# Loading the second attention tile ahead of the weights, by halves of the heads, in a fused attention and MLP kernel

## The chip, the cores and the metric

The kernel runs on one core of a Trainium2 chip. The time is device microseconds of one execution; medians over several executions are given. In the profile PE is the engine of matrix products (PEld its weight loads), DVE, ACT and POOL are the vector, scalar and general engines, and SP issues DMAs.

## The reference

```python
scores = (q @ k.T) / sqrt(64)              # q, k, v: [4, 8, 768, 64], float32
# retrieval heads: causal mask; others: causal and (first 4 keys or last 64 keys)
a = softmax(where(mask, scores, -1e9))
x = (a @ v) as [3072, 512]                 # the heads side by side
h = x @ w_in                               # [512, 2048]
out = (h - tanh(h)) @ w_out                # [2048, 512] -> [3072, 512]
```

## The kernel before

The 3072 tokens are cut into 12 tiles of 256. A tile has four head pairs. For each pair: transposes of q and k (`tp`), copies of them (`qT`, and two `kz`), scores (`sc`), exp (`pt`), a mask multiply with `m`, the product with v (`av`), a division (`x`), a transpose back (`xp`) and a copy (`xT`). A bank in the code is one of a few output buffers of PE that the steps use in turn. Then come the tile's MLP (the two products with `w_in` and `w_out`), `ph` (with `w_in`), `th`, `gt` and `po` (with `w_out`), with the attention of later tiles in its gaps. All instructions are recorded with an estimated cost, and a planner in the kernel (`Plan`) simulates them to choose a fixed order for each engine.

```python
    def load(t, names="qkv"):                  # SP queue: q, k, v of tile t
        ...
            for i in range(NB):                # NB = 2 blocks of 128 tokens
                op("SP", 420, lambda ...: nc.sync.dma_start(
                        out=r()[:, i, :, :],
                        in_=src[b, :, s0 : s0 + 128, :].rearrange("h p d -> p h d")),
                    w=[("raw", idx, i)], dma=(1024, 21.0))
    def load_w_in(j):                          # POOL queue: fp32 to fp16 on the way
        ...
            r=[("v1", 0, 0)], w=[("win", j)], dma=(512, 80.0))
    def load_w_out(j):
        ...
            r=[("v1", 0, W_OUT_AFTER)], w=[("wout", j)], dma=(512, 80.0))
    # ... cut: constants, masks m4, casts, scores, av
    def st_X(n):
        ...
        xp, key = bank([128, NB, 128], FP16, "m", f"xp{n}")   # av uses "m" too: one bank
    # ... cut: MLP units
    cast_qk(0, (("DVE", "DVE"), ("DVE", "ACT")))
    cast_v(0)
    for j in range(4):
        load_w_in(j)
    scale_v(0)
    load(1)
    for n in range(HP):                        # the four head pairs of tile 0
        st_T(n, "ACT", ("DVE", "DVE"))
        # ... cut: scores, av and xp of the pairs before
    cast_qk(1, (("DVE", "DVE"), ("DVE", "POOL")))
    cast_v(1)
    scale_v(1)
    for j in range(4):
        load_w_out(j)
    load(2)
```

The softmax here doesn't subtract the row's maximum and nothing guards it: scores larger than these inputs give would overflow.

Of the kernel before, what the change touches and what calls it, by code (L numbers as in the profile page):

```python
# [7 lines left out]
FP32 = mybir.dt.float32  # L8
# [4 lines left out]
TT = 256  # L13
# [3 lines left out]
class Plan:  # L17
# [15 lines left out]
    def op(self, eng, ns, fn, r=(), w=(), dma=None, prio=None):  # L33
# [18 lines left out]
        self.ops.append((eng, ns, fn, deps, dma, i if prio is None else prio))  # L52
        return i

    def run(self):
# [15 lines left out]

        def enqueue(i):
            queue[self.ops[i][0]].append(i)

        def finish(i, done):
            self.done[i] = done
            e, ns, _, _, dma, _ = self.ops[i]
# [14 lines left out]
        while len(order) < n:  # L92
            t, e = min(
                [(max(free[e], min(ready[i] for i in q)), e) for e, q in queue.items() if q],
# [18 lines left out]
            elif nxt < t:  # L113
# [4 lines left out]
                (i for i in queue[e] if ready[i] <= t), key=lambda i: self.ops[i][5]  # L118
            )
            queue[e].remove(i)  # L120
            _, ns, _, _, dma, _ = self.ops[i]
            self.start[i] = t
            order.append(i)
            free[e] = t + max(ns - self.OVERLAP[e], 40)
            if dma:
                packets, each = dma
                rings["POOL" if e == "POOL" else "SP"].append(
                    [i, t + ns + 300, each, packets * each / 16]
                )
            else:  # L130
                finish(i, t + ns + self.RESULT[e])
# [6 lines left out]
def kernel(  # L138
# [86 lines left out]
    def load(t, names="qkv"):  # L225
        b, g = divmod(t, NG)
        for nm in names:
            src = {"q": q, "k": k, "v": v}[nm]
            idx = 3 * t + "qkv".index(nm)
            r = lazy(raw_pool, [128, NB, H, D], FP32, "raw", f"raw_{nm}{t}")  # L230
            for i in range(NB):
                s0 = g * TT + i * 128
                op(
                    "SP", 420,
                    lambda r=r, i=i, src=src, s0=s0: nc.sync.dma_start(
                        out=r()[:, i, :, :],
                        in_=src[b, :, s0 : s0 + 128, :].rearrange("h p d -> p h d"),
                    ),
                    w=[("raw", idx, i)], dma=(1024, 21.0),
                )  # L240
            raws[nm, t] = (r, idx)

    W_OUT_AFTER = 2
# [3 lines left out]
    def load_w_in(j):  # L247
# [7 lines left out]
            r=[("v1", 0, 0)], w=[("win", j)], dma=(512, 80.0),  # L255
# [3 lines left out]
    def load_w_out(j):  # L259
# [7 lines left out]
            r=[("v1", 0, W_OUT_AFTER)], w=[("wout", j)], dma=(512, 80.0),  # L267
# [12 lines left out]
    load(0, "qk")  # L280
    load(0, "v")
# [80 lines left out]
    for h in range(H):  # L362
# [6 lines left out]
            r=["thr", "A4", "A40", "A41", "A43"], w=[("m4", h // 2)],  # L369
# [15 lines left out]
    def cast_qk(t, engines):  # L385

        for nm, es in zip("qk", engines):
            c = lazy(t16_pool, [128, NB, H, D], FP16, f"t16{nm}", f"t16_{nm}{t}")
            r, slot = raws[nm, t]
            for i, e in enumerate(es):  # L390

                def fn(c=c, r=r, i=i, e=e):
                    if e == "ACT":
                        nc.scalar.copy(out=c()[:, i, :, :], in_=r()[:, i, :, :])
                    else:
                        engs[e].tensor_copy(out=c()[:, i, :, :], in_=r()[:, i, :, :])  # L396

                op(
                    e, {"ACT": 590, "DVE": 380, "POOL": 540}[e], fn,
                    r=[("raw", slot, i)], w=[("t16" + nm, t, i)],  # L400
                )
            t16s[nm, t] = c
# [4 lines left out]
    def cast_v(t):  # L407
        b, g = divmod(t, NG)
        if g == 0:
            v1s[b] = lazy(v_pool, [128, 2 * NG, H, D + 1], FP16, "v1", f"v1_{b}")  # L410
            vfs[b] = lazy(v_pool, [128, 4, H, D + 1], FP16, "vf", f"vf_{b}")
        v1, vf, lo = v1s[b], vfs[b], g * NB
        r, slot = raws["v", t]
        op(
            "POOL", 200,
            lambda: nc.gpsimd.memset(v1()[:, lo : lo + NB, :, D : D + 1], 1.0 / XS),
            w=[("v1", b, lo + i) for i in range(NB)],
        )
        for i in range(NB):
            op(  # L420
                "POOL", 540,
                lambda i=i: nc.gpsimd.tensor_copy(  # L422
                    out=v1()[:, lo + i, :, 0:D], in_=r()[:, i, :, :]
                ),
                r=[("raw", slot, i)], w=[("v1", b, lo + i)],
            )

    def scale_v(t):
        b, g = divmod(t, NG)
        v1, vf, lo = v1s[b], vfs[b], g * NB  # L430
        for jb in range(lo, min(lo + NB, 4)):
# [7 lines left out]
                r=[("v1", b, jb), "rflag0", "rflag"], w=[("vf", b, jb)],  # L439
# [6 lines left out]
    xTs = {}  # L446

    def st_T(n, eq="DVE", ek=("DVE", "DVE")):
# [6 lines left out]
        def mm():  # L455
# [9 lines left out]
            r=["ident"] + [("t16" + nm, t, i) for nm in "qk" for i in range(NB)], w=[key],  # L465
        )
        qT[n] = lazy(qt_pool, [128, TT], FP16, f"qT{hp}", f"qT{n}")

        def copy(e, dst, src):
            if e == "ACT":  # L470
                nc.scalar.copy(out=dst, in_=src)  # L471
            else:
                nc.vector.tensor_copy(out=dst, in_=src)  # L473
# [33 lines left out]
    def st_S(n, gi):  # L507
# [35 lines left out]
        if gi == 0:  # L543
# [15 lines left out]
            op("DVE", 560 if g == 0 else 695, mask, r=pk + [("m4", hp)], w=pk)  # L559
# [3 lines left out]
    def st_A(n, i):  # L563
# [20 lines left out]
        r += [("v1", b, jb) for jb in range(max(qb - 1, 0), qb + 1)]  # L584
# [20 lines left out]
    def st_X(n):  # L605
# [3 lines left out]
        xp, key = bank([128, NB, 128], FP16, "m", f"xp{n}")  # L609

        def mm():
            for i in range(NB):
# [6 lines left out]
            "DVE", 290,  # L619
            lambda: nc.vector.tensor_copy(  # L620
                out=xTs[t]()[:, hp, :], in_=xp()[:].rearrange("p i c -> p (i c)")
            ),
# [103 lines left out]

    cast_qk(0, (("DVE", "DVE"), ("DVE", "ACT")))
    cast_v(0)
    for j in range(4):
        load_w_in(j)  # L730
    scale_v(0)
    load(1)
# [100 lines left out]
```

## Time and profile before

| | before |
|---|---|
| median of 3 runs (range) | 276.85 us (276.75 to 277.22) |
| profiled span | 275.6 us |
| PE busy / idle | 251.2 / 24.4 us |
| PE idle from 0 to 48 us | 18.8 us |
| first w_in issued; last w_out landed | 10.44; 48.2 us |
| first `ph` | 23.94 us |
| last `xp` of tile 1 | 46.91 us |

The stage table, the timeline (start, duration, engine, line, operation, count; in brackets the idle time ahead of it and what ended it) and the queue rows are in the prediction below. These are PE rows of the timeline of the kernel before (start, duration, engine, line, operation, count; in brackets the idle time ahead of it and what ended it):

```profile
39.72 0.19 PE L578 MATMUL av<-vf,pt 128*128 128x65 f16 x1 [0.90 <-DVE xT L620]
...
46.91 0.29 PE L613 MATMUL xp<-ident,x 128*128 128x128 f16 x2 [0.73 <-DVE x L597]
```

Tile 1's attention, which waits on DVE for each pair, then has little beside it to fill PE: tile 0's `ph` is over by 36.3 us, and only `po` rows, from 40.91 on, stand between its pairs.

### The profile page before, as it was taken

To read this page: it belongs to the slowest core of one execution; us is meant where nothing else is said; L and a number is where in the kernel's file an instruction comes from. 1 tells how busy PE (TensorE), PEld (TensorE's weight loads), DVE (VectorE), ACT (ScalarE), POOL (GpSimd) and SP (SyncE) were. 2 spreads that over 40 slices of the span, in tenths; PEclk is the share of its full clock that TensorE was granted. 3 is DMA by queue.
4 is the path that set the end of the run, shared out by engine and by line. 5 is a ranking of instruction groups with operands and counts; after the bars stand their busy time and mean duration, and the time that the engine had idled before them with its cause. 6 is when DMAs were issued, how large, how long until landed. Compare 5 with 4: busy or idle time off the path is not lost.

```text
span 275.6 us, 6251 instructions
## 1 busy us (share of the span) xinstructions
PE 251.2 (91%) x2560; PEld 186.9 (68%) x2560; DVE 179.6 (65%) x452; ACT 154.2 (56%) x223; POOL 69.5 (25%) x116
## 2 busy tenths in 40 slices
PE   0457977999999999999999999999999999999984
PEld 0335764888778777777777777777777877776631
DVE  7784775776898875556987655567987655554310
ACT  2330464788357676665476776564567566644420
POOL 7530940527190730206803000300300000000000
PEclk9999999999999999999999999999999999999999
DMA  7999999999989590182860210010001001011101
GB/s 140 217 199 209 191 207 203 221 220 232 230 177 201 129 224 32 40 190 66 201 144 15 76 43 4 37 40 38 2 38 40 2 38 40 1 40 39 40 38 76
DMA packets 82733, 29.78 MB, mean 108 GB/s; under 512 B 75536, under 2 KB 79632, under 8 KB 82704
## 3 DMA queue, kind: packets, MB, share of 16 engines
q1 hardware_dynamic: 78336, 25.17, 41.7%
q0 software_dynamic: 4224, 4.19, 9.2%
q8 instruction: 20, 0.33, 0.5%
q14 instruction: 9, 0.07, 0.1%
q10 hardware_dynamic: 144, 0.01, 0.0%
HBM read 27.27 MB, written 6.29 MB: 122 GB/s over the span
## 4 chain that ended last, share of the span: by engine, by line
PE 84%; DVE 11%; ACT 2%; issue 2%
PE ph L642 29%; PE po L678 29%; PE sc L522 13%; PE av L578 8%; PE tp L458 3%; PE xp L613 2%; DVE x L597 1%; DVE kz L473 1%; DVE gt L662 1%; DVE pt L554 1%; DVE pt L549 1%; DVE kz L331 1%; DVE m L365 1%; DVE xT L620 1%; ACT th L655 1%
## 5 line engine op out<-in xcount | busy, mean ns | idle before, releaser
L642 PE MATMUL ph<-xT,win 128*128 128x256 f16 x768 | 103.3, 278 | 0.7 <-DVE gt L662 0.7
L678 PE MATMUL po<-wout,gt 128*128 128x512 f16 x384 | 100.0, 379 | 1.4 <-ACT ot L691 1.4
L537 ACT ACTIVATE pt<-sc 128x1024 f16<-128x1024 f32 (+1 forms) x96 | 85.5, 916 | 23.7 <-PE sc L522 19.4
L655 ACT ACTIVATE th<-ph 128x512 f32<-128x512 f32 x96 | 57.4, 598 | 71.4 <-PE ph L642 67.5
L662 DVE SCALAR_TENSOR_TENSOR gt<-th,ph 128x512 f16<-128x512 f32 x96 | 65.8, 686 | 38.6 <-ACT th L655 38.1
L642 PEld LDWEIGHTS <-win 128*128 128x128 f16 x768 | 73.8, 100 | 16.3 <-issue 1.1
L522 PE MATMUL sc<-qT,kz 128*128 128x128 f16 (+1 forms) x448 | 53.2, 250 | 2.5 <-DVE kz L473 2.0
L678 PEld LDWEIGHTS <-gt 128*128 128x128 f16 x384 | 34.2, 98 | 23.3 <-issue 1.9
L522 PEld LDWEIGHTS <-kz 128*128 128x128 f16 x448 | 37.0, 99 | 14.1 <-DVE kz L473 2.8
L578 PEld LDWEIGHTS <-pt 128*128 128x128 f16 x672 | 30.1, 98 | 9.6 <-issue 2.1
L396 POOL CAST t_q<-raw_q 128x512 f16<-128x512 f32 x20 | 12.4, 646 | 90.3 <-PE tp L458 47.5
L578 PE MATMUL av<-v,pt 128*128 128x65 f16 x352 | 29.3, 196 | 1.5 <-DVE xT L620 0.8
L473 DVE COPY kz<-tp 64x256 f16<-64x256 f16 x96 | 27.1, 283 | 3.4 <-ACT qT L471 1.2
L554 DVE TENSOR_TENSOR pt<-pt,m 128x1024 f16<-128x1024 f16 x32 | 23.3, 729 | 4.7 <-ACT pt L537 4.7
L578 PE MATMUL av<-vf,pt 128*128 128x65 f16 x320 | 23.5, 193 | 1.6 <-DVE xT L620 0.9
L458 PE MATMUL tp<-ident,t_q 128*128 128x128 f16 x96 | 13.8, 226 | 9.2 <-DVE t_q L396 8.8
L691 ACT ACTIVATE ot<-po 128x512 f32<-128x512 f32 x24 | 14.4, 598 | 12.9 <-PE po L678 12.7
L597 DVE TENSOR_TENSOR x<-av,rinv 128x256 f16<-128x256 f32 x48 | 20.3, 423 | 1.5
L592 DVE RECIPROCAL rinv<-av 128x4 f32<-128x4 f32 x48 | 8.7, 180 | 17.7 <-PE av L578 17.2
L422 POOL CAST v<-raw_v 128x512 f16<-128x512 f32 x24 | 15.0, 641 | 18.7 <-DMA raw_v<-in_v_dram 18.5
L435 POOL TENSOR_TENSOR vf<-v,rflag 128x520 f16<-128x520 f16 x16 | 18.2, 1146 | 0.7
L458 PEld LDWEIGHTS <-t_q 128*128 128x128 f16 x96 | 8.8, 101 | 13.4 <-DVE t_q L396 8.9
(35 smaller groups left out, 121.7 us busy)
## 6 DMA issues: line engine op xcount, KB each, us to landing
raw_q<-in_q_dram SPq DMA_DIRECT2D x24, 256.0 KB, 4.9
raw_k<-in_k_dram SPq DMA_DIRECT2D x24, 256.0 KB, 4.8
raw_v<-in_v_dram SPq DMA_DIRECT2D x24, 256.0 KB, 4.9
out_dram<-ot SPq DMA_DIRECT2D x24, 256.0 KB, 2.1
win<-in_moe_w_in_dram POOLq DMA_DIRECT2D x4, 512.0 KB, 10.4
wout<-in_moe_w_out_dram POOLq DMA_DIRECT2D x4, 512.0 KB, 10.6
retr_i<-in_is_retrieval_dram ACTq DMA_DIRECT2D x1, 8.0 KB, 3.1
```

The source lines that it names most:

```text
L435: lambda jb=jb, fl=fl: nc.gpsimd.tensor_mul(out=vf()[:, jb, :, :], in0=v1()[:, jb, :, :], in1=fl[:].unsqueeze(2).to_broadcast([128, H, D + ...
L458: nc.tensor.transpose(out=tp()[:, x, i, :], in_=c()[:, i, 2 * hp : 2 * hp + 2, :], identity=ident16[:],)
L473: nc.vector.tensor_copy(out=dst, in_=src)
L522: nc.tensor.matmul(out=sc()[:, hh, o : o + nb * 128], lhsT=kk[:, hh, jb * 128 : jb * 128 + 128], rhs=qT[n]()[:, q0 * 128 : (q0 + nb) * 128 ...
L537: lambda: nc.scalar.activation(out=pt()[:, :, 512 * gi : 512 * gi + wid], in_=sc()[:, :, 0:wid], func=AF.Exp, scale=inv_sqrt_d,),
L554: nc.vector.tensor_mul(out=pv, in0=pv, in1=m4[:, hs, 256:512].unsqueeze(2).to_broadcast([128, 2, 2, 256]),)
L578: nc.tensor.matmul(out=av()[:, i, hh, :], lhsT=pt()[:, hh, co : co + 128], rhs=vv()[:, jb, h, :], start=(jb == 0), stop=(jb == qb),)
L597: lambda: nc.vector.tensor_mul(out=x16()[:], in0=av()[:, :, :, 0:D], in1=rinv()[:].unsqueeze(3).to_broadcast([128, NB, 2, D]),),
L642: nc.tensor.matmul(out=ph()[:, j, :], lhsT=w_in_t[fb // 4]()[:, cb, f0 : f0 + 128], rhs=xTs[t]()[:, cb, :], start=(cb == 0), stop=(cb == H ...
L655: lambda: nc.scalar.activation(out=th()[:], in_=ph()[:], func=AF.Tanh, scale=1.0 / XS),
L662: lambda: nc.vector.scalar_tensor_tensor(out=gts[t]()[:, u * FU : (u + 1) * FU, :], in0=th()[:], scalar=-XS, in1=ph()[:], op0=ALU.mult, op ...
L678: nc.tensor.matmul(out=po()[:], lhsT=gts[t]()[:, f, ts * 128 : ts * 128 + 128], rhs=w_out_t[f // 4]()[:, f % 4, :], start=(f == 0), stop=( ...
```

## The change

The intent is that PE should have two tiles' attention to work on before the MLP starts. Tile 1's q, k, v are requested, moved and cast before the weights; loads and casts go by halves of the heads, so that the first pairs can start on half a tile; two copies move to ACT; `xp` of tile 0 uses the bank `o`, idle until the first `po`. The planner also learns that DVE and POOL share a port.

```diff
-    def load(t, names="qkv"):
+    def load(t, names="qkv", halves=(None,)):
     ...
-            r=[("v1", 0, 0)], w=[("win", j)], dma=(512, 80.0),
+            r=w_after, w=[("win", j)], dma=(512, 80.0),
     ...
-    load(0, "qk")
-    load(0, "v")
+    for half in range(2):
+        load(0, "qk", (half,))
+        load(0, "v", (half,))
     ...
-    cast_qk(0, (("DVE", "DVE"), ("DVE", "ACT")))
-    cast_v(0)
-    for j in range(4):
-        load_w_in(j)
-    scale_v(0)
-    load(1)
+    cast_qk(0, (("DVE", "DVE"), ("ACT", "DVE")), (0,))
+    cast_v(0, ("POOL", "POOL"), (0,))
+    cast_qk(0, (("DVE", "DVE"), ("DVE", "DVE")), (1,))
+    cast_v(0, ("POOL", "POOL"), (1,))
+    load(1, halves=range(2))
     for n in range(HP):
-        st_T(n, "ACT", ("DVE", "DVE"))
+        st_T(n, "ACT", ("DVE", "ACT"))
     ...
-            st_X(n - 3)
+            st_X(n - 3, "o")
     ...
-    cast_qk(1, (("DVE", "DVE"), ("DVE", "POOL")))
-    cast_v(1)
+    for half in range(2):
+        cast_qk(1, (("POOL", "POOL"), ("ACT", "POOL")), (half,))
+        cast_v(1, ("POOL", "POOL"), (half,))
+    for j in range(4):
+        load_w_in(j, [("t16k", 1, 1)])
+    load(2)
+    scale_v(0)
     scale_v(1)
     for j in range(4):
-        load_w_out(j)
-    load(2)
+        load_w_out(j, [("v1", 0, 1, 1)])
```

Cut: the planner's port, and the bookkeeping of halves.

More of the change, by code (lines that the diff above doesn't have):

```diff
@@ L31, in __init__, with op @@
         self.readers = {}
-    def op(self, eng, ns, fn, r=(), w=(), dma=None, prio=None):
+    def op(self, eng, ns, fn, r=(), w=(), dma=None, prio=None, port=False):
         i = len(self.ops)
@@ L51, in op @@
         deps.discard(i)
-        self.ops.append((eng, ns, fn, deps, dma, i if prio is None else prio))
+        port = port or (eng == "POOL" and not dma)
+        self.ops.append((eng, ns, fn, deps, dma, i if prio is None else prio, port))
         return i
@@ L70, in run, with at @@
         order = []
+        self.port = 0.0
+        def at(i):
+            return max(ready[i], self.port) if self.ops[i][6] else ready[i]
         def enqueue(i):
@@ L76, in finish @@
             self.done[i] = done
-            e, ns, _, _, dma, _ = self.ops[i]
+            e, ns = self.ops[i][:2]
             for u in users[i]:
@@ L93, in run @@
             t, e = min(
-                [(max(free[e], min(ready[i] for i in q)), e) for e, q in queue.items() if q],
+                [(max(free[e], min(at(i) for i in q)), e) for e, q in queue.items() if q],
                 default=(1e12, None),
@@ L117, in run @@
             i = min(
-                (i for i in queue[e] if ready[i] <= t), key=lambda i: self.ops[i][5]
+                (i for i in queue[e] if at(i) <= t), key=lambda i: self.ops[i][5]
             )
             queue[e].remove(i)
-            _, ns, _, _, dma, _ = self.ops[i]
+            _, ns, _, _, dma, _, port = self.ops[i]
             self.start[i] = t
@@ L124, in run @@
             free[e] = t + max(ns - self.OVERLAP[e], 40)
+            if port:
+                self.port = free[e]
             if dma:
@@ L223, with load_w_in @@
     raws = {}
-    def load(t, names="qkv"):
+    HH = H // 2
+    def load(t, names="qkv", halves=(None,)):
         b, g = divmod(t, NG)
-        for nm in names:
-            src = {"q": q, "k": k, "v": v}[nm]
-            idx = 3 * t + "qkv".index(nm)
-            r = lazy(raw_pool, [128, NB, H, D], FP32, "raw", f"raw_{nm}{t}")
-            for i in range(NB):
-                s0 = g * TT + i * 128
-                op(
-                    "SP", 420,
-                    lambda r=r, i=i, src=src, s0=s0: nc.sync.dma_start(
-                        out=r()[:, i, :, :],
-                        in_=src[b, :, s0 : s0 + 128, :].rearrange("h p d -> p h d"),
-                    ),
-                    w=[("raw", idx, i)], dma=(1024, 21.0),
-                )
-            raws[nm, t] = (r, idx)
-    W_OUT_AFTER = 2
+        for half in halves:
+            h0, nh = (0, H) if half is None else (half * HH, HH)
+            for nm in names:
+                src = {"q": q, "k": k, "v": v}[nm]
+                if (nm, t) not in raws:
+                    idx = rot["raw"] = rot.get("raw", -1) + 1
+                    raws[nm, t] = (
+                        lazy(raw_pool, [128, NB, H, D], FP32, "raw", f"raw_{nm}{t}"), idx
+                    )
+                r, idx = raws[nm, t]
+                for i in range(NB):
+                    s0 = g * TT + i * 128
+                    op(
+                        "SP", max(420, 128 * nh * 1.1),
+                        lambda r=r, i=i, src=src, s0=s0, h0=h0, nh=nh: nc.sync.dma_start(
+                            out=r()[:, i, h0 : h0 + nh, :],
+                            in_=src[b, h0 : h0 + nh, s0 : s0 + 128, :].rearrange("h p d -> p h d"),
+                        ),
+                        w=[("raw", idx, i, x) for x in (range(2) if half is None else (half,))],
+                        dma=(128 * nh, 21.0),
+                    )
     w_in_t = []
     w_out_t = []
-    def load_w_in(j):
+    def load_w_in(j, w_after):
         w = lazy(w_pool, [128, HP, 512], FP16, f"win{j}", f"win{j}")
@@ L254, in load_w_in, with load_w_out @@
             ),
-            r=[("v1", 0, 0)], w=[("win", j)], dma=(512, 80.0),
+            r=w_after, w=[("win", j)], dma=(512, 80.0),
         )
         w_in_t.append(w)
-    def load_w_out(j):
+    def load_w_out(j, w_after):
         w = lazy(w_pool, [128, 4, DM], FP16, f"wout{j}", f"wout{j}")
@@ L266, in load_w_out @@
             ),
-            r=[("v1", 0, W_OUT_AFTER)], w=[("wout", j)], dma=(512, 80.0),
+            r=w_after, w=[("wout", j)], dma=(512, 80.0),
         )
@@ L368 @@
             ),
-            r=["thr", "A4", "A40", "A41", "A43"], w=[("m4", h // 2)],
+            r=["thr", "A4", "A40", "A41", "A43"], w=[("m4", h // 2)], port=True,
         )
@@ L383, with cast_op @@
     t16s = {}
-    def cast_qk(t, engines):
-        for nm, es in zip("qk", engines):
-            c = lazy(t16_pool, [128, NB, H, D], FP16, f"t16{nm}", f"t16_{nm}{t}")
-            r, slot = raws[nm, t]
-            for i, e in enumerate(es):
-                def fn(c=c, r=r, i=i, e=e):
-                    if e == "ACT":
-                        nc.scalar.copy(out=c()[:, i, :, :], in_=r()[:, i, :, :])
-                    else:
-                        engs[e].tensor_copy(out=c()[:, i, :, :], in_=r()[:, i, :, :])
-                op(
-                    e, {"ACT": 590, "DVE": 380, "POOL": 540}[e], fn,
-                    r=[("raw", slot, i)], w=[("t16" + nm, t, i)],
+    def cast_op(e, ns, dst, src, r, w):
+        cost = {"ACT": 163 + 0.85 * ns, "DVE": 85 + 0.65 * ns, "POOL": 90 + 0.96 * ns}[e]
+        if e == "ACT":
+            op(e, cost, lambda: nc.scalar.copy(out=dst(), in_=src()), r=r, w=w)
+        else:
+            op(e, cost, lambda: engs[e].tensor_copy(out=dst(), in_=src()), r=r, w=w, port=True)
@@ new lines, in cast_qk @@
+    def cast_qk(t, engines, halves=range(2)):
+        for half in halves:
+            for nm, es in zip("qk", engines):
+                if (nm, t) not in t16s:
+                    t16s[nm, t] = lazy(
+                        t16_pool, [128, NB, H, D], FP16, f"t16{nm}", f"t16_{nm}{t}"
+                    )
+                c = t16s[nm, t]
+                r, slot = raws[nm, t]
+                hs = slice(half * HH, half * HH + HH)
+                cast_op(
+                    es[half], NB * HH * D, lambda c=c, hs=hs: c()[:, :, hs, :],
+                    lambda r=r, hs=hs: r()[:, :, hs, :],
+                    r=[("raw", slot, i, half) for i in range(NB)], w=[("t16" + nm, t, half)],
@@ L401, in cast_qk, with cast_v @@
                 )
-            t16s[nm, t] = c
     v1s = {}
     vfs = {}
-    def cast_v(t):
+    def cast_v(t, engines=("POOL", "POOL"), halves=range(2)):
         b, g = divmod(t, NG)
-        if g == 0:
+        lo = g * NB
+        if b not in v1s:
             v1s[b] = lazy(v_pool, [128, 2 * NG, H, D + 1], FP16, "v1", f"v1_{b}")
             vfs[b] = lazy(v_pool, [128, 4, H, D + 1], FP16, "vf", f"vf_{b}")
-        v1, vf, lo = v1s[b], vfs[b], g * NB
+        v1 = v1s[b]
         r, slot = raws["v", t]
-        op(
-            "POOL", 200,
-            lambda: nc.gpsimd.memset(v1()[:, lo : lo + NB, :, D : D + 1], 1.0 / XS),
-            w=[("v1", b, lo + i) for i in range(NB)],
-        )
-        for i in range(NB):
-            op(
-                "POOL", 540,
-                lambda i=i: nc.gpsimd.tensor_copy(
-                    out=v1()[:, lo + i, :, 0:D], in_=r()[:, i, :, :]
-                ),
-                r=[("raw", slot, i)], w=[("v1", b, lo + i)],
+        for half in halves:
+            hs = slice(half * HH, half * HH + HH)
+            op(
+                "POOL", 150,
+                lambda hs=hs: nc.gpsimd.memset(v1()[:, lo : lo + NB, hs, D : D + 1], 1.0 / XS),
+                w=[("v1", b, g, half)],
+            )
+            cast_op(
+                engines[half], NB * HH * D, lambda hs=hs: v1()[:, lo : lo + NB, hs, 0:D],
+                lambda hs=hs: r()[:, :, hs, :],
+                r=[("raw", slot, i, half) for i in range(NB)], w=[("v1", b, g, half)],
@@ L438, in scale_v @@
                 ),
-                r=[("v1", b, jb), "rflag0", "rflag"], w=[("vf", b, jb)],
+                r=[("v1", b, g, 0), ("v1", b, g, 1), "rflag0", "rflag"], w=[("vf", b, jb)],
             )
@@ L446, with copy @@
     xTs = {}
+    def copy(e, dst, src):
+        if e == "ACT":
+            nc.scalar.copy(out=dst, in_=src)
+        else:
+            nc.vector.tensor_copy(out=dst, in_=src)
     def st_T(n, eq="DVE", ek=("DVE", "DVE")):
@@ L464, in st_T @@
             "PE", 224, mm,
-            r=["ident"] + [("t16" + nm, t, i) for nm in "qk" for i in range(NB)], w=[key],
+            r=["ident"] + [("t16" + nm, t, hp * 2 // HP) for nm in "qk"], w=[key],
         )
         qT[n] = lazy(qt_pool, [128, TT], FP16, f"qT{hp}", f"qT{n}")
-        def copy(e, dst, src):
-            if e == "ACT":
-                nc.scalar.copy(out=dst, in_=src)
-            else:
-                nc.vector.tensor_copy(out=dst, in_=src)
         cost = {"ACT": 373, "DVE": 288}
@@ L557, in mask @@
                     )
-            op("DVE", 560 if g == 0 else 695, mask, r=pk + [("m4", hp)], w=pk)
+            op("DVE", 560 if g == 0 else 695, mask, r=pk + [("m4", hp)], w=pk, port=True)
     avs = {}
@@ L583, in st_A @@
         r = [("pt", n, gi) for gi in range(len(GROUPS[g]))]
-        r += [("v1", b, jb) for jb in range(max(qb - 1, 0), qb + 1)]
+        r += [("v1", b, gg, hp * 2 // HP) for gg in range(max(qb - 1, 0) // NB, g + 1)]
         r += [("vf", b, jb) for jb in range(qb - 1)]
@@ L603, in st_A, with st_X @@
             x16s[n] = x16
-    def st_X(n):
+    def st_X(n, tag="m", eng="DVE"):
         t, hp = divmod(n, HP)
@@ L608, in st_X @@
             xTs[t] = lazy(xt_pool, [128, HP, TT], FP16, "xT", f"xT{t}")
-        xp, key = bank([128, NB, 128], FP16, "m", f"xp{n}")
+        xp, key = bank([128, NB, 128], FP16, tag, f"xp{n}")
         def mm():
@@ L618, in st_X @@
         op(
-            "DVE", 290,
-            lambda: nc.vector.tensor_copy(
-                out=xTs[t]()[:, hp, :], in_=xp()[:].rearrange("p i c -> p (i c)")
-            ),
+            eng, {"ACT": 373, "DVE": 290}[eng],
+            lambda: copy(eng, xTs[t]()[:, hp, :], xp()[:].rearrange("p i c -> p (i c)")),
             r=[key], w=[("xT", t, hp)],
@@ L747 @@
         st_A(n, 1)
-        st_X(n - 1)
-    st_X(HP - 1)
-    cast_qk(1, (("DVE", "DVE"), ("DVE", "POOL")))
-    cast_v(1)
+        st_X(n - 1, "o")
+    st_X(HP - 1, "o")
+    for half in range(2):
[5 more added lines that the diff above has]
+    scale_v(0)
     scale_v(1)
     for j in range(4):
-        load_w_out(j)
-    load(2)
+        load_w_out(j, [("v1", 0, 1, 1)])
     for hp in range(HP):
```

## The prediction

> **What bounds the kernel now.** I read the page first (busy shares, slices), then the stage table, the timeline and chain of the first 50 us, and the DMA queues.
>
> ```profile
> span 275.6 us, 6251 instructions
> ...
> PE 251.2 (91%) x2560; PEld 186.9 (68%) x2560; DVE 179.6 (65%) x452; ACT 154.2 (56%) x223; POOL 69.5 (25%) x116
> ...
> PE   0457977999999999999999999999999999999984
> ```
>
> TensorE (PE) is busy 91% of the time, and its slices are full from the eighth on. The stages:
>
> ```profile
> 0.00:9.05 9.05, 0.29 (x1) 0.10 (x2) 7.61 (x21) 1.89 (x3) 5.12 (x21) 1.00 0.84 160
> 9.05:23.94 14.89, 8.41 (x63) 5.50 (x64) 10.13 (x26) 4.85 (x9) 7.21 (x9) 1.00 1.25 203
> 23.94:33.00 9.06, 8.69 (x58) 6.49 (x57) 4.68 (x7) 3.21 (x6) 5.01 (x7) 1.00 1.13 209
> 33.00:48.23 15.23, 12.09 (x148) 8.64 (x145) 10.97 (x32) 8.28 (x11) 5.43 (x8) 1.00 1.19 200
> 48.23:263.70 215.47, 214.54 (x2267) 163.18 (x2265) 146.18 (x368) 134.80 (x194) 46.74 (x72) 1.00 0.40 91
> ```
>
> Columns: stretch, its length, then busy us of PE, PE weight loads, DVE, ACT, POOL, the clock, the DMA share, GB/s. From 48.23 to 263.70 PE idles 0.9 us in 215: nothing but less PE work could help there, and the change removes none. Before 48.23 PE idles 18.7 us (9.05 - 0.29, 14.89 - 8.41, 9.06 - 8.69, 15.23 - 12.09). After 263.7 come the last rows, which the change does not touch. So the change can win only in the first 50 us, and what it wins there comes off the end one for one, if PE then stays full.
>
> ```profile
> 6.47 2.19 DVE L365 TENSOR_SCALAR m<-A,thr 128x512 f16<-128x512 f16 x8
> 8.65 0.62 ACT L394 CAST t_k<-raw_k 128x512 f16<-128x512 f32 x1 [5.90 <-DMA raw_k<-in_k_dram]
> 10.44 0.95 POOL L251 DMA_DIRECT2D win<-in_moe_w_in_dram  x1
> 12.99 1.40 DVE L549 TENSOR_TENSOR pt<-pt,m 128x768 f16<-128x768 f16 x1
> 19.42 0.29 DVE L620 COPY xT<-xp 128x256 f16<-128x256 f16 x1
> 19.76 0.49 PE L578 MATMUL av<-v,pt 128*128 128x65 f16 x6 [0.38 <-DVE xT L620]
> 21.77 0.49 PE L578 MATMUL av<-v,pt 128*128 128x65 f16 x6 [0.38 <-DVE xT L620]
> 22.83 0.61 POOL L396 CAST t_k<-raw_k 128x512 f16<-128x512 f32 x1 [6.34 <-DMA raw_k<-in_k_dram]
> 23.94 6.36 PE L642 MATMUL ph<-xT,win 128*128 128x256 f16 x32
> ```
>
> Three things to see. Tile 0 waits for the whole of k (ACT, until 8.65). Then av, x, xp and xT share the one "m" bank: av of each later head pair waits for the xT copy of an earlier one, 2.01 us apart (19.76, 21.77). And the weights, issued at 10.44, push tile 1's k back to 22.83, so PE has nothing but tile 0's MLP for 24 to 32.
>
> **What the Trainium skill says.** "TensorE: Matmul & The Clock Gate", Part 1: the array starts at half clock and is released after some 3.4 us of activity. The trace agrees: the 32 ph matmuls at 23.94 take 199 ns each, later groups of eight take 0.87 us, 109 ns each. The clock row shows 1.00 throughout, so it is no witness here. "DMA: Bandwidth & Descriptors", Queues, rings and completion order: each DMA engine takes turns between queues packet by packet. The trace agrees, and says what that means for these sizes (16 to 24 us):
>
> ```profile
> q0 software_dynamic: 1225, 1.21, 89.1%
> q1 hardware_dynamic: 1495, 0.38, 32.9%
> ```
>
> Packets are about equal, bytes are not: the weights (q0) get 1.21 MB in 8 us, 0.151 MB/us; q, k, v (q1) get 0.38 MB, 0.048 MB/us. Alone, q1 moved 1.78 MB in the 8 us from 4 to 12, 0.22 MB/us. "SBUF — State Buffer", SBUF: two separate sides: DVE and POOL lock a shared port pair against each other. The mask multiply took 1.40 us beside POOL, 0.56 us elsewhere, which fits.
>
> **The change, part by part** (times from here are estimates).
>
> (a) Halves of the heads. The first pairs need q and k of four heads, 0.52 MB, not 1.05. At 0.22 MB/us that is some 2.4 us earlier: k at about 6.2. But the order on DVE now puts the eight m instructions (2.19 us, from about 6.1) ahead of the first cast of q: it ends at about 8.7, and the first transposes start at 8.8, against 9.05 (q) and 9.38 (k). Gain 0.5 us, not 2.4.
>
> (b) Copies and banks in tile 0. One kz copy of each pair moves from DVE to ACT, and xp takes the "o" bank, idle until the first po. The av to av cycle loses xp (0.40) and xT (0.29) and their hand-overs, some 0.8 of 2.0 us, and becomes bound by ACT and DVE. By my count of DVE's 17 instructions from the first kz to the last x of the third pair, 6.0 us of work, plus port locks, the last av of tile 0 comes at 18.3, against 21.77. Gain 3.5 us.
>
> (c) Tile 1 ahead of the weights. w_in is now issued after tile 1's last k cast, in POOL's order behind the v casts and two vf multiplies. Bytes ahead of it: tile 0 (1.57 MB), tile 1's first half (0.79), q and k of the second (0.52), 2.88 MB. q1 had 0.29 + 0.91 + 0.87 = 2.07 MB at 12.0 in before; the remaining 0.81 at 0.22 end at 15.7, and land some 1.35 us later (half of v, 1.31 MB, was moved by 8.5 and taken at 9.88). Cast 0.61: first w_in issue T = 17.8, 7.4 us later than before.
>
> (d) When weights land. In before the four w_in landed 7.0 us (first) to 17.8 us (last issued at 13.4, 14.8 to land) after the first issue, about 3.5 us apart. The four w_out follow in the same queue without a gap now, as POOL issues them at about 25 to 28: w_in at 25.0, 28.4, 31.8, 35.6, w_out at 38.8, 42.2, 45.6, 49.1. In before the last w_out landed at 33.7 + 14.5 = 48.2: the end of the weights hardly moves. Tile 2's q and k (0.68 of 1.05 MB moved before w_in starts, the rest at 0.048) are there by 30, in time.
>
> (e) PE through tile 1. With its q and k cast by 16 to 18, tile 1's pairs follow tile 0's at once. Each needs ACT 1.02 + 0.81, DVE about 2.4, and PE at half clock; three pairs of scores and two of av from 18.5 bring the first ph to 27 to 29, w_in being there. In before it was 23.94, but with no tile 1 done. The 8 ph units alternate with th and gt on two banks (0.87 + 0.60 + 0.69 and hand-overs, two in flight, 1.25 us each) and with the last pair: tile 0's ph ends at 38 to 39.5.
>
> (f) The point where both orders have the same work left. In the changed order, after the fourth w_out block is used in tile 0's first rows (matmul 344 of PE's order), what is left equals that after matmul 360 of the old order within 0.1 us: 8 ph more (0.87), 22 av and 2 xp less (0.77). Old time: 56.3. New: from 38.5, 5.5 ph units (4.8), 16 po (3.45), tile 2's tp, scores (2.4) make 10.7, so 49.2 if no wait; the last w_out at 49.1 plus four po 0.9 gives 50.0; with PE at 39.5 and a microsecond or two of bank and ACT waits, 51 to 52. I take 51.4: gain 5.0. Then PE is full as before.
>
> Sum: 276.85 - 5.0 = 271.9. Checked by parts: 4.0 from (a) and (b), and about 4 from tile 1 being ready instead of arriving behind the weights, less 3 because PE reaches the first ph later and follows the weights' landing.
>
> **Rivals.** (1) Weights become the bound: T slips by port locks on POOL (seven POOL instructions stand close before it), every landing slips with it, and PE waits at ph or po. For it: landing and need are within 1 us at w_in 3 and w_out 3. Each us of T is then a us; with T at 20 the gain is 2.5 us, 274.3. (2) The early PE idle is filled better than I think: the array warms during the denser tile 1 stage and the bank cycle hides behind attention; then only the last w_out rules, gain 6.4, 270.4, or more if q1 pauses and the weights go faster: 269. (3) It is hidden anyway: tile 1's work merely swaps places with tile 0's MLP and the last w_out, which moves from 48.2 to 49.1, sets the point; then about 276 to 277. Against it: in before PE stands 56.3 - 48.2 = 8 us behind the last landing, so the landing wasn't its bound.
>
> **Range and chances.** Terms: T plus or minus 1 us, (e) plus or minus 1.5, (f) 1. Together: 268.6 to 275.0 for 8 in 10. The 2% line is 271.3 us, just under my centre: faster 0.40, within 2% 0.57, slower 0.03.
>
> **What would show it.** First transposes at about 8.8 behind the m group; av groups of tile 0 no longer released by xT and the last near 18.3; first w_in issue near 17.8; first ph at 27 to 29, at nearly 109 ns per matmul rather than 199; PE waits on w_in or w_out, if rival 1 holds; PE idle before 48 down from 18.7 to 13 or 14; later stages alike. I am wrong if ph starts after 31, if T is past 20, or if PE idles again after 52.

## The result

The changed kernel takes 272.24 us in the median of four runs. Three lie at 272.05 to 272.34; the fourth, at 279.62, is left out of the ratio (the median of the three is 272.13). Executions over 1.5% slower than the fastest of the same kernel are left out of the means. Before, on the same chip, takes 276.80. All ratios here are the mean time of one kernel's fast runs over the mean of the other's of the same rounds, so not quite the ratio of the quoted medians: 0.983, with a 95% interval of 0.981 to 0.985. It is 1.7% faster, inside the 2% band. The profiled span fell from 275.6 to 270.5 us.

The page of the changed kernel, to set beside the first fence of the prediction:

```profile
span 270.5 us, 6313 instructions
...
PE 249.0 (92%) x2560; PEld 187.1 (69%) x2560; DVE 174.7 (65%) x445; ACT 156.9 (58%) x228; POOL 71.3 (26%) x130
...
PE   0477889999999999999999999999999999999974
```

PE's busy time fell by 2.2 us and its idle time by 2.9 (24.4 to 21.5): together the 5.1 us of the span. The stage table of the changed kernel, in the columns of the prediction:

```profile
9.05:23.94 14.89, 11.14 (x86) 7.86 (x87) 9.88 (x30) 8.18 (x15) 11.75 (x15) 1.00 1.31 214
23.94:33.00 9.06, 7.19 (x100) 6.12 (x99) 6.12 (x17) 5.41 (x8) 4.95 (x8) 1.00 1.22 197
33.00:48.23 15.23, 13.63 (x135) 11.13 (x132) 9.85 (x21) 8.52 (x15) 1.18 (x2) 1.00 1.22 201
...
60.00:259.00 199.00, 198.22 (x2070) 149.84 (x2067) 132.92 (x340) 122.27 (x177) 40.12 (x69) 1.00 0.37 85
```

From 9 to 24 us PE has 11.14 us of work in place of 8.41; from 24 to 33 it idles 1.5 us more than before, and does 100 matmuls in 7.19 us where before did 58 in 8.69 (48 of those are `ph`; many of the 100 are smaller). After 60 us PE is full, as before. The timeline of the changed kernel (rows picked):

```profile
5.98 2.75 DVE L383 TENSOR_SCALAR m<-A,thr 128x512 f16<-128x512 f16 x8
6.23 0.62 ACT L406 CAST t_k<-raw_k 128x512 f16<-128x512 f32 x1 [3.47 <-DMA raw_k<-in_k_dram]
...
9.12 0.39 PE L487 MATMUL tp<-ident,t_q 128*128 128x128 f16 x2 [9.12 <-DVE t_q L408]
...
11.48 1.44 PE L545 MATMUL sc<-qT,kz 128*128 128x256 f16 x8 [1.33 <-ACT kz L473]
...
17.62 0.95 POOL L268 DMA_DIRECT2D win<-in_moe_w_in_dram  x1
...
19.64 1.10 DVE L572 TENSOR_TENSOR pt<-pt,m 128x768 f16<-128x768 f16 x1
...
20.80 0.51 PE L601 MATMUL av<-v,pt 128*128 128x65 f16 x6 [0.80 <-DVE pt L572]
...
29.94 1.91 PE L663 MATMUL ph<-xT,win 128*128 128x256 f16 x16
...
37.74 0.27 PE L636 MATMUL xp<-ident,x 128*128 128x128 f16 x2
```

The first half of k is there at 6.2, but PE starts at 9.12, behind the group of eight `m` instructions. `ph` comes 6 us later than before and is warm, that is, at about 109 ns each: the group of 16 takes 1.91 us. In before most of the first 32 are cold, at about twice that: 6.36 us for 32. Tile 1's last `xp` now stands at 37.74 us instead of 46.91. PE's waits from 8 to 60 us (waited for: us in total, times, longest):

```profile
PE tp L487 <- DVE t_q L408: 9.1, 1, 9.1
PE xp L636 <- DVE x L620: 1.7, 2, 1.0
PE sc L545 <- ACT kz L473: 1.3, 1, 1.3
```

The four rows left out (`av` twice, `ph`, `tp`) are of 1.1 us and less, and none of the seven names a weight's DMA. The DMA queues of the changed kernel from 26 to 30 us (packets, MB, share):

```profile
q0 software_dynamic: 616, 0.61, 90.3%
q1 hardware_dynamic: 617, 0.15, 29.7%
```

Tile 2's load runs beside the weights, packet for packet, and with a quarter of the bytes.

### The profile page after: what moved, and what is told of

It is laid out like the page before. It is cut to its first block, busy times and chain, and to the rows that moved or that the text cites. A ratio compares the mean times of both kernels' runs of the same rounds, so it can differ in the third digit from the quotient of the medians.

```text
span 270.5 us, 6313 instructions
## 1 busy us (share of the span) xinstructions
PE 249.0 (92%) x2560; PEld 187.1 (69%) x2560; DVE 174.7 (65%) x445; ACT 156.9 (58%) x228; POOL 71.3 (26%) x130
## 4 chain that ended last, share of the span: by engine, by line
PE 86%; DVE 7%; ACT 4%; issue 2%; DVEq 0%
PE po L699 30%; PE ph L663 29%; PE sc L545 14%; PE av L601 8%; PE tp L487 4%; ACT pt L560 2%; PE xp L636 2%; DVE gt L683 1%; DVE pt L572 1%; DVE kz L349 1%; DVE m L383 1%; ACT th L676 1%; DVE x L620 1%; ACT ot L712 1%; DVE nz L359 0%
## 5 line engine op out<-in xcount | busy, mean ns | idle before, releaser
L663 PE MATMUL ph<-xT,win 128*128 128x256 f16 x768 | 100.7, 273 | 0.9 <-DVE gt L683 0.9
L663 PEld LDWEIGHTS <-win 128*128 128x128 f16 x768 | 71.9, 98 | 14.1 <-issue 1.2
L545 PE MATMUL sc<-qT,kz 128*128 128x128 f16 (+1 forms) x448 | 54.1, 255 | 1.5 <-ACT kz L473 1.3
L545 PEld LDWEIGHTS <-kz 128*128 128x128 f16 x448 | 38.6, 101 | 13.8 <-issue 1.5
L408 POOL CAST t_q<-raw_q 128x512 f16<-128x512 f32 x22 | 13.5, 625 | 82.6 <-issue 41.1
L475 DVE COPY kz<-tp 64x256 f16<-64x256 f16 x92 | 26.0, 283 | 2.2 <-ACT qT L473 1.1
```

What stands on the lines that cost most here:

```text
L408: op(e, cost, lambda: engs[e].tensor_copy(out=dst(), in_=src()), r=r, w=w, port=True)
L475: nc.vector.tensor_copy(out=dst, in_=src)
L545: nc.tensor.matmul(out=sc()[:, hh, o : o + nb * 128], lhsT=kk[:, hh, jb * 128 : jb * 128 + 128], rhs=qT[n]()[:, q0 * 128 : (q0 + nb) * 128 ...
L663: nc.tensor.matmul(out=ph()[:, j, :], lhsT=w_in_t[fb // 4]()[:, cb, f0 : f0 + 128], rhs=xTs[t]()[:, cb, :], start=(cb == 0), stop=(cb == H ...
```

## The experiments

Twelve more kernels ran; all gave correct results. Three kernels spread more than the others: win_early (275.97 to 279.25), win_later (271.44 to 274.5) and start_early (270.43 to 272.17). Each diff is against the changed kernel unless it says otherwise. The ratios are to before.

| kernel | median us | ratio (95%) | first w_in issue | first `ph` |
|---|---|---|---|---|
| changed | 272.24 | 0.983 (0.981 to 0.985) | 17.62 | 29.94 |
| xp_in_m | 271.74 | 0.981 (0.979 to 0.983) | 17.30 | 28.62 |
| win_early | 277.32 | 1.002 (0.998 to 1.006) | 11.72 | 24.73 |
| whole_loads | 270.86 | 0.979 (0.976 to 0.981) | 16.19 | 26.03 |
| cast_first | 272.42 | 0.984 (0.982 to 0.986) | 17.42 | 30.23 |
| old_win_late | 272.63 | 0.983 (0.982 to 0.985) | 16.43 | 27.55 |
| win_later | 272.57 | 0.985 (0.982 to 0.988) | 18.39 | 29.75 |
| kz_dve | 273.79 | 0.989 (0.988 to 0.990) | 17.22 | 30.74 |
| whole_m | 270.35 | 0.977 (0.976 to 0.978) | 16.35 | 25.55 |
| pe_order | 270.80 | 0.978 (0.976 to 0.980) | 17.40 | 28.95 |
| tile1_whole | 275.55 | 0.995 (0.993 to 0.997) | 16.21 | 30.91 |
| start_early | 271.00 | 0.979 (0.976 to 0.982) | 16.10 | 26.72 |
| vf_apart | 274.07 | 0.991 (0.989 to 0.992) | 16.09 | 28.48 |

### win_early: the weights first again

```diff
-        load_w_in(j, [("t16k", 1, 1)])
+        load_w_in(j, [("v1", 0, 0, 1)])
```

> The changed kernel with one part undone: w_in is issued once tile 0's v is cast, near 12 us, ahead of tile 1's loads in effect, since the weights' queue takes three quarters of the bytes. My theory (tile 1's q and k arriving before the weights is what fills PE): tile 1's last k cast moves from 17.1 to 25 or later, PE idles again between 25 and 45, and the time is 275 to 276.5 us. Rival (only the end of the last weight block counts, and that hardly moves): 271.5 to 272.7.

Measured: 277.32 us, the whole gain gone and a little more than the 275 to 276.5 expected, with every other part of the change kept. The profile is of a run of 277.8 us. Its stage from 33 to 48 us:

```profile
33.00:48.00 15.00, 11.08 (x104) 8.15 (x103) 8.09 (x22) 5.92 (x9) 4.26 (x8) 0.77 1.17 194
```

Tile 1's attention is again alone at the end (last `xp` 45.86, as 46.91 in before), PE idles 3.9 us there, and the granted clock falls to 0.77, and `xp` takes 0.42 us in place of 0.28. Three of the six runs show a clock of 0.994 and 275.97 to 276.85 us, three 0.987 to 0.988 and 277.8 to 279.25; the profile with its cold stretch is one of the latter. One expectation missed: tile 1's last cast of k was at 20.95, not after 25, as the loads had a lead on the weights. It is tile 1's v that came late: POOL waited 6.01 us for it and cast its second half at 27.57 (18.56 in the changed kernel). But tile 1's third pair begins (`tp`) only at 36.00, after tile 0's last `ph`, which is where the planner had put it. How much of the loss is late data and how much is the order that the planner makes for it, no run separates. And the run is not a pure one: a mask multiply took 3.07 us beside POOL, after which PE had idled 2.31 us before an `av` of tile 0, so up to half of the 5.1 us loss may come from that. The next run does not have this flaw.

### old_win_late: that part alone, in the kernel before

Against the kernel before:

```diff
-            r=[("v1", 0, 0)], w=[("win", j)], dma=(512, 80.0),
+            r=[("t16k", 1, 1)], w=[("win", j)], dma=(512, 80.0),
...
     cast_v(0)
-    for j in range(4):
-        load_w_in(j)
...
     cast_v(1)
+    for j in range(4):
+        load_w_in(j)
```

> The kernel before with one part of the change done alone: w_in is issued after tile 1's last k cast instead of after tile 0's first v cast. No halves, no o bank, no copies moved to ACT, casts as before. My theory after the first four runs (the order of loads is the whole gain, because tile 1's attention then runs beside tile 0's MLP instead of after it): first w_in issue near 16.5 us, 270.3 to 272.0 us. Rival (the order needs the other parts with it): 273.5 to 276.

Measured: 272.63 us (271.69 to 272.89), ratio 0.983, as the full change, though above the 270.3 to 272.0 expected. No halves, no second bank, no copies moved. Its last `av` of tile 0 stands at 22.75 us, even later than before's 21.77 and 2 us later than in the changed kernel, and costs nothing that shows, because tile 1's last `xp` is at 38.53:

```profile
16.43 0.95 POOL L251 DMA_DIRECT2D win<-in_moe_w_in_dram  x1
...
27.55 1.91 PE L642 MATMUL ph<-xT,win 128*128 128x256 f16 x16
...
38.53 0.28 PE L613 MATMUL xp<-ident,x 128*128 128x128 f16 x2
```

What PE got done by 48 us (columns of the stage table; the first number in brackets counts its matmuls) shows it too. Before, then changed, then old_win_late:

```profile
0.00:48.00 48.00, 29.24 (x261) 20.54 (x262) 33.39 (x84) 18.22 (x27) 22.77 (x44) 1.00 1.13 195
```

```profile
0.00:48.00 48.00, 31.73 (x311) 24.88 (x312) 33.42 (x84) 23.98 (x38) 23.84 (x52) 1.00 1.17 196
```

```profile
0.00:48.00 48.00, 32.00 (x314) 25.17 (x315) 35.85 (x89) 21.41 (x33) 22.38 (x44) 0.93 1.16 197
```

The order of the weights alone moves 53 matmuls into this stretch. Matmuls differ in size; in PE's busy time, what is left after 48 us is 222.0, 217.3 and 217.0 us (busy time of the whole span less the first 48). So this part alone gives as much as the whole change, and what the other parts gain and lose about cancels. The part includes the new order that the planner makes once it knows that the weights come later.

### win_later: does T still rule?

T is the prediction's name for the time of the first w_in issue.

```diff
-        load_w_in(j, [("t16k", 1, 1)])
+        load_w_in(j, [("v1", 0, 1, 1)])
```

> The changed kernel with w_in issued one cast later, after tile 1's last v cast: T about 19 instead of 17.6, all eight weight blocks 1.4 us later. My theory (in the changed kernel every block landed 2 to 4.7 us before PE took it, so they are no bound): within 0.5 us of 272.2. Rival (the landings pace PE): 273.4 to 274. The planner also moves some of PE's order, so a small difference either way may be that.

Measured: the issue moved by 0.77 us only (18.39), and the time is 272.57 us, with a spread of 271.44 to 274.5. The effect, if any, is inside the spread. The run neither shows nor excludes that a later T costs its own length.

### xp_in_m: the o bank undone

```diff
-            st_X(n - 3, "o")
+            st_X(n - 3)
...
-        st_X(n - 1, "o")
-    st_X(HP - 1, "o")
+        st_X(n - 1)
+    st_X(HP - 1)
```

> The changed kernel with one part undone: tile 0's x transposes go through the m bank again. My theory (the bank chain was part of tile 0's length, 0.7 us per pair, but other waits now stand beside it): 0.5 to 1.5 us slower than the changed kernel, 272.7 to 273.7 us; av groups of tile 0 again released by xT. Rival (the bank was the whole gain): 275 to 277. Rival (the bank gives nothing, the kz and mask waits set tile 0's length): within 0.3 us of 272.2.

Measured: 271.74 us, 0.5 faster than with the bank, which none of the three expectations had. The second bank does let the transposes of tile 0 go earlier (`xp` at 16.15, 17.27, 19.58, 22.22 against 17.18, 19.75, 22.87, 24.43), but that reaches no later point. The 0.5 us may be the order's (see pe_order): here too the planner put the first `ph` ahead of the fourth pair's `tp`.

### cast_first: the first cast of q ahead of the masks

```diff
-    for h in range(H):          # the eight m instructions, 2.7 us of DVE
-        op("DVE", 260, ...)
...
     cast_qk(0, (("DVE", "DVE"), ("ACT", "DVE")), (0,))
+    for h in range(H):
+        op("DVE", 260, ...)
```

> The changed kernel with the eight m instructions placed behind the first cast of q in DVE's order. My theory (DVE's order threw away 2 us of the halves' gain, and the weights have some 2 us of slack behind PE): first transposes at about 7.0 instead of 9.1, first scores near 9.5 instead of 11.5, 1 to 2 us faster than the changed kernel, 270.2 to 271.2 us, with PE now just behind the last weight block (landing at 49). Rival (tile 1's data or the weights set the pace from 17 us on): within 0.4 us of 272.2.

Measured: 272.42 us, no gain, as the rival said. Timeline of this kernel:

```profile
6.19 2.74 DVE L743 TENSOR_SCALAR m<-A,thr 128x512 f16<-128x512 f16 x8
...
6.33 0.40 PE L478 MATMUL tp<-ident,t_q 128*128 128x128 f16 x2 [6.33 <-DVE t_q L399]
...
8.85 0.47 DVE L466 COPY kz<-tp 64x256 f16<-64x256 f16 x2
...
10.15 1.44 PE L536 MATMUL sc<-qT,kz 128*128 128x256 f16 x8 [2.67 <-ACT kz L464]
```

PE starts 2.8 us earlier, the scores 1.3 us earlier (10.15, not 11.48), as the copies of k now queue behind the masks on DVE; the first `av` 0.9 (13.06, not 13.95), and the third scores are 0.45 us later than in the changed kernel (15.38, 14.93). The head start dies within three pairs: DVE has the same work to do by then, in another order.

### kz_dve: the copy of k back on DVE

```diff
-        st_T(n, "ACT", ("DVE", "ACT"))
+        st_T(n, "ACT", ("DVE", "DVE"))
```

> The changed kernel with one part undone: both kz copies of tile 0's pairs on DVE again. My theory (the two engines take turns on one bank, so the copy moved to ACT comes third in a row on it and shortens nothing: the first scores waited on ACT's kz): first scores at 10.9 to 11.5 instead of 11.48, within 0.5 us of 272.2, more likely faster. Rival (DVE is tile 0's bound and needs the relief): 273 to 274.

Measured: 273.79 us, 1.55 slower: my theory was wrong, and the time is in the rival's range. The first scores do come earlier (11.01, not 11.48), but PE then idles 5.05 us from 9 to 24 us instead of 3.8, and the first `ph` is at 30.74. PE's waits in this stretch are mostly for DVE (1.2 us for the mask multiply, 1.2 for `kz`, 1.0 for `x`), which fits the rival. Shown it is not: 1.55 us is hardly more than what a mere change of the order gives (pe_order below).

### whole_loads and whole_m: no halves

whole_loads; whole_m has the edit of xp_in_m as well:

```diff
-    for half in range(2):
-        load(0, "qk", (half,))
-        load(0, "v", (half,))
+    load(0, "qk")
+    load(0, "v")
...
-    load(1, halves=range(2))
+    load(1)
```

> The changed kernel with one part undone: tiles 0 and 1 are loaded as whole tiles of eight heads, casts still by halves. My theory (the m group on DVE held the first cast of q to 8.65 us, by which time all of k is in, so halves buy little at the start; v and tile 1 come a little later): 0.3 to 1.2 us slower, 272.5 to 273.4; first transposes still at 9.1 to 9.4. Rival (halves carry the gain): 274 to 276.5.

> Two parts undone together, each of which was faster without: whole loads of tiles 0 and 1, and x transposes of tile 0 in the m bank. If the two add up: 270.86 - 0.5 = 270.4 us; if they fill the same idle time of PE: 270.7 to 271.0; if one needs the other: 271.5 or more. A version below 271.3 beats the kernel before by 2%.

Measured: 270.86 and 270.35 us. The first is a miss: a loss of 0.3 to 1.2 us was expected, and 1.4 were won. The second is where the two gains add up. whole_m is the fastest kernel, 2.3% faster than before. From its timeline:

```profile
6.29 2.19 DVE L382 TENSOR_SCALAR m<-A,thr 128x512 f16<-128x512 f16 x8
...
8.88 0.39 PE L486 MATMUL tp<-ident,t_q 128*128 128x128 f16 x2 [8.88 <-DVE t_q L407]
```

Tile 0's four mask multiplies as a group of DVE (count, busy us, mean ns, idle before them), first of whole_m from 12 to 26 us, then of the changed kernel from 9 to 24:

```profile
L571 DVE TENSOR_TENSOR pt<-pt,m 128x768 f16<-128x768 f16 x4 | 2.5, 625 | 0.7 <-ACT pt L559 0.5
```

```profile
L572 DVE TENSOR_TENSOR pt<-pt,m 128x768 f16<-128x768 f16 x4 | 3.5, 874 | 1.8 <-ACT pt L560 1.8
```

Whole loads start no later (8.88, not 9.12): in the changed kernel the early half of v lets POOL cast in the midst of the `m` group, which takes 2.75 us in place of 2.19, and its masks take 874 ns each in place of 625. So the halves bring no earlier start and cost DVE time. How much of the 1.4 us is that, and how much the order of instructions, the next runs ask; they don't settle it.

### pe_order: another order, the same transfers

```diff
-            r=w_after, w=[("win", j)], dma=(512, 80.0),     # in load_w_in
+            r=w_after, w=[("win", j)], dma=(512, 70.0),
```

This number is only the planner's belief of how fast w_in moves. The orders of POOL and SP, and so all DMAs, stay word for word the same. PE's order first differs where a `ph` comes ahead of the fourth pair's `tp` of tile 1, and DVE's and ACT's follow.

> The changed kernel with nothing different but the order that the planner writes down: it is told that w_in blocks take a little less time, so the first ph group and two later ones come one to three groups earlier in PE's order, before a tp or an av; the DMA and POOL orders are the same line for line. My theory (a part of what separates the variants at 271 to 272 is only where the first ph groups stand in PE's fixed order, as they fill PE's waits for DVE and ACT): 0.3 to 1.0 us faster than 272.2. Rival (the DMA times decide): within 0.2 us of 272.2.

Measured: 270.80 us, 1.4 faster than the changed kernel with the same operations, and more than the 0.3 to 1.0 expected. The traces bear out that the work of POOL and SP comes in the same order in both. In this one:

```profile
28.95 1.91 PE L663 MATMUL ph<-xT,win 128*128 128x256 f16 x16
30.69 0.28 PE L487 MATMUL tp<-ident,t_q 128*128 128x128 f16 x2
```

In the changed kernel these `tp` start at 29.72, ahead of the `ph`. So the order alone is worth as much as whole loads are, and no difference of up to 1.4 us between two kernels that the planner ordered differently can be put down to an edit on the time alone.

### tile1_whole and vf_apart: tile 0 by halves, tile 1 whole

tile1_whole, then vf_apart on top of it:

```diff
-    load(1, halves=range(2))
+    load(1)
```

```diff
-    scale_v(1)                      # two multiplies on POOL, right after w_in
...
+                if t == 1:          # after tile 2's casts
+                    fs.append(lambda: scale_v(1, [("t16k", 2, 1)]))
```

> The changed kernel with halves kept for tile 0 and tile 1 loaded whole. If the halves of tile 1 are what cost (its v of the first half stands ahead of q and k of the second, so the last k and w_in come 1.2 us later): T near 16.2 and 270.6 to 271.2 us, as with both tiles whole (270.86). If it was the halves of tile 0: 271.9 to 272.5.

> The kernel of tile1_whole with one thing moved: the second pair of scaling multiplies of v on POOL (needed only by tile 2) is held back until tile 2's last cast of k, so that POOL no longer runs two of them back to back behind its casts of v while VectorE does tile 0's last mask multiplies. Theory (the loss of tile1_whole is that one mask multiply, which took 3.06 us beside POOL): the mask multiplies of tile 0 take 0.55 to 1.1 us each again, the 2.58 us gap of PE before tile 0's last av is gone, and the time is 271.0 to 272.8 us. Rival (the loss comes from loading tile 1 whole, or from the order of PE): 275.0 to 275.6 us, as in tile1_whole, with or without the long mask.

tile1_whole: 275.55 us, 3.3 slower and outside both expectations, though w_in was issued 1.4 us earlier. From its timeline:

```profile
20.03 3.06 DVE L572 TENSOR_TENSOR pt<-pt,m 128x768 f16<-128x768 f16 x1
...
20.60 2.07 POOL L458 TENSOR_TENSOR vf<-v,rflag 128x520 f16<-128x520 f16 x2
...
23.15 0.51 PE L601 MATMUL av<-v,pt 128*128 128x65 f16 x6 [2.58 <-DVE pt L572]
```

The mask multiply that takes 0.55 us elsewhere took 3.06 and ended just after POOL's two multiplies (20.60 + 2.07 = 22.67). vf_apart takes these away from there. From its timeline:

```profile
20.75 0.55 DVE L572 TENSOR_TENSOR pt<-pt,m 128x768 f16<-128x768 f16 x1
...
21.35 0.51 PE L601 MATMUL av<-v,pt 128*128 128x65 f16 x6
```

The mask is back to 0.55 us and PE's wait before that `av` is gone, so POOL's two multiplies are shown to have held up that mask. But the time is 274.07 us, between the two expectations: 1.5 us of the 3.3 came back. PE's idle time fell by 1.6 us (23.8 to 22.2 over the span, near the 21.5 of the changed kernel) and its busy time rose by 0.6 (249.6 to 250.2). What is left against the changed kernel, 1.8 us by the medians, is in the profiles 0.7 us more idle and 1.2 us more busy time of PE. Its cause was not isolated; orders differ, and pe_order has shown that as much as 1.4 us can come from that.

### start_early: an attempt at a better version

Halves for tile 0 alone, `xp` in its old bank, and the masks split: two `m` after the first cast of q, six after the first copies of k.

```diff
     cast_qk(0, (("DVE", "DVE"), ("ACT", "DVE")), (0,))
+    m4_ops((0, 1))
...
         st_T(n, "ACT", ("DVE", "ACT"))
+        if n == 1:
+            m4_ops(range(2, H))     # these wait for the first kz
```

> Attempt at a faster version: halves for tile 0 alone, tile 1 whole, x transposes in the m bank, the first cast of q ahead of the m group on DVE, and six of the eight m instructions behind the first two kz copies. My theory: first transposes at 6.4, first scores near 8.5 instead of 11.3, tile 0 over 1 to 2 us earlier, but tile 1's k (cast by 16) and the last weight block (landing near 47) leave little of it: 269.6 to 270.4 us against 270.35 for the best so far. If the early start carries through: below 269.4. If it is all lost: 270.4 to 271.2.

Measured: 271.00 us, where all of the early start is lost, and no better than whole_m at 270.35, which stays the fastest. The early start did come: first transposes at 6.57 (8.88 in whole_m) and the last `av` of tile 0 at 19.63 (21.58). But the first `ph` came at 26.72 (25.55).

## Why the prediction was right or wrong

The time was right: 271.9 predicted, 272.24 measured, on the side of the 2% line that was given the larger chance. The steps were not all right, and some errors offset each other: that the number came this close is in part luck.

(a) First transposes: 8.8 predicted, 9.12 measured. The `m` group in the way was seen; its lengthening from 2.19 to 2.75 us beside POOL's early cast of v was not. Gain from halves: none (9.05 before).

(b) Tile 0's last `av`: 18.3 predicted, 20.80 measured. This step failed by its size. Two terms were too small: the first scores come only at 11.48, as the three copies of one `tp` bank go one after the other on two engines (the scores wait 1.33 us on ACT's `kz`), and the four masks took 0.73, 0.72, 0.95 and 1.10 us where 0.56 and some port time had been reckoned. And the head start would have been worth little: old_win_late has this point at 22.75 and the same time. So the check by parts, "4.0 from (a) and (b)", named the wrong source. Undoing the bank alone gained 0.5 us, and doing without the halves 1.4, both no more than what the order alone can do.

(c) First w_in issue: 17.8 predicted, 17.62 measured. (d) Landings of w_in, 25.0 to 35.6 predicted, were 25.2 to 35.5, and of w_out, 38.8 to 49.1, were 38.9 to 49.0. Counting bytes ahead of the request, and taking rates for each queue from the trace of before, was good to 0.2 us.

(e) First `ph`: 27 to 29 predicted, 29.94 measured, mostly (b)'s 2.5 us carried on. The last 16 of tile 0's 64 `ph` begin at 38.43 and end at 40.4; 38 to 39.5 was predicted.

(f) Common point of the two orders: 51.4 predicted, 51.99 measured, against 56.34 before. Of the lateness of (b) and (e), only 0.6 us arrived here: the allowance of "a microsecond or two of bank and ACT waits" was not used up. From the end of tile 0's `ph` at 40.4 PE idled only 0.5 us to this point. The gain at this point is 4.35 us; the medians' is 4.6.

PE idle before 48 us: 13 to 14 predicted, 16.3 measured. So of the 5 us of idle time that the prediction wanted to save, 2.5 were saved. The rest of the gain is busy time: the first `ph` are no longer at half rate, and the group of all `ph` fell from 103.3 to 100.7 us. The prediction named that among its signs but not as a gain of its own. Its "the trace agrees" on the clock holds for the half rate, not for the 3.4 us: in before the first 26 `ph` start 213 ns apart, with no gap for over 5 us, before the next are at 109.

Rival 1, that the weights become the bound: not seen. The first w_in landed 4.7 us before the first `ph`, the last w_out 2.1 us before the `po` that uses it (49.0, 51.13), and PE waits for no weight. Moving T by 0.77 us gave no clear answer. The prediction's figure for T at 20, 274.3, does not follow from its own sums: T later by 2.2 us turns the 50.0 that the last weight allows in (f) into 52.2, a gain of about 4 and not 2.5. Rival 2: the warm array came true, the rest not, as the idle time was longer. Rival 3, that it is hidden anyway, is refuted by the time.

What explains the gain, in one sentence: with the weights behind tile 1, tile 1's attention, which waits on DVE and ACT between its pairs, has tile 0's `ph` to fill PE beside it, while in before `ph` ran first, alone and cold, and that attention had little beside it from 36 to 47 us. That the later weights, with the order that the planner makes for them, are the cause is shown by doing that part alone (272.63) and, with the flaw told there, by undoing it (277.32). How it acts is read from the traces; no run keeps the early weights and puts tile 1's attention ahead in PE's order, so whether the order of the transfers or that of PE counts more stays open.

## What to carry to other kernels

When the first megabytes are all wanted at once, move first what makes work that waits (attention on three engines), and last what makes work that fills (long runs of matmuls), as long as it lands before it is used. Do the part that you believe in alone, on the old kernel: it may be the whole gain. And where a planner orders the engines, first measure what a mere reordering does; here it was 1.4 us, about as much as any part but the order of the weights.

## What the Trainium skill lacked or had wrong

- "TensorE: Matmul & The Clock Gate", Part 1: it warns that the clock events of a trace can be unreliable, but not that the granted clock of a profile can miss a cold start altogether. In before that figure is 1.00 from 24 to 33 us while the 32 `ph` took 199 ns each, against 109 warm; in win_early, where PE went cold again, it read 0.77. The durations are the witness.
- "DMA: Bandwidth & Descriptors", Queues, rings and completion order: it has the turns by packets, not what they do to bytes. Here 616 packets of one queue carried 0.61 MB while 617 of the other carried 0.15; in before, q, k and v fell from 0.22 MB/us alone to 0.048 beside the weights.
- "SBUF — State Buffer", SBUF: two separate sides: it says that the later instruction waits for the one that holds the port pair. It doesn't say that two in a row can be sat out, nor that this can befall the one that began first. A 0.55 us multiply on DVE took 3.06 us in tile1_whole and 3.07 in win_early, and ended 0.42 us after the second of POOL's two multiplies in both, though its record begins 0.57 and 0.56 us before the first of them.
- No page tells what the order alone of the same instructions is worth: here 1.4 us of 272 with the same operations and transfers (pe_order).
